# Sigmoid attention and an MLP on one core: blocks of 512 tokens, 64-row scores, float32 products with v, and engine queues written out from a list of tasks

## The chip, the core and the metric

The kernel runs on one core of a Trainium2 chip. The core has TensorE (PE in the profile, with its weight loads as PEld), VectorE (DVE), ScalarE (ACT), GpSimd (POOL, unused here) and SyncE (SP), which issues all DMA transfers. Each engine works through its own queue in order, and engines wait for one another by semaphores. The metric is the device time of one execution in microseconds, the median of several runs.

## The reference

```python
batch, n_heads, seq, head_dim = (8, 12, 448, 64)
scores = scale * np.matmul(q, k.transpose(0, 1, 3, 2)) - np.log(S)     # scale = 1 / sqrt(64), S = 448
attn = 1.0 / (1.0 + np.exp(-scores))
attn_out = np.matmul(attn, v)
x = attn_out.transpose(0, 2, 1, 3).reshape(B * S, H * D)               # 3584 tokens x 768
h = x @ w_in                                                           # w_in 768 x 2048, float64
g = h * (1.0 / (1.0 + np.exp(-1.702 * h)))
out = (g @ w_out).astype(np.float32)                                   # w_out 2048 x 768, float64
```

q, k and v are float32. The weights come to the device as 64-bit words and have to be turned into float32 there.

## The kernel before

**Number formats.** TensorE takes float32 data in two ways here: as fp32r, a rounded format in which one pass does the product, or as plain float32, which the profile shows as two records per product. To keep precision in fp32r, a value is split into a rounded high part and a low part (value minus high part), and a product is the sum of three: low times high, high times low, high times high. Rounding is a copy into an fp32r tile (ScalarE or VectorE), the low part a subtraction on VectorE.

**Weights.** The two matrices are cut into 32 pieces of 128 x 768. The words of a piece are decoded once (`decode_steps`: exponent, bounds, mantissa, low, sign, product; lines 118 to 149) and the float32 result is stored in DRAM (`saved`). The decoding steps are dealt out over the attention of the first batch and the first MLP by `emit`. For each of the 8 batches every piece is loaded (`load_w`, line 161) and split again (`split_w`, lines 168 and 169) into a `wsplit` tile.

**Attention.** It goes head by head. For the first 15 pairs of heads (`NATIVE`) the scores of a chunk of 128 keys are two products on all 128 rows: the high and low parts of k are stacked on the two halves of the rows against q. The probabilities stay float32 and `values_whole` (line 333) multiplies them by v in float32, the two heads of a pair on the two column halves of the array. The other 33 pairs have probabilities and v split into high and low parts (line 313), the scores take seven wide products per head (line 289), and so do the products with v (`values`, line 355), with high and low v side by side on the 128 columns.

**MLP.** It goes batch by batch, on 448 tokens: 16 pieces up (`up`, line 429: 6 k-tiles x 3 products each), sigmoid, product with h, split; then 6 output tiles down (`down`, line 454: 16 x 3 products each). One batch is 576 products of 128 x 128 weights with 448 columns.

**Order.** TensorE's queue is written by hand: attention of the first six pairs comes first, then each batch's MLP with the attention of later pairs dealt between its products (`interleave`, `PAIRS`). SP's queue is by hand in the first part. All the other queues are ordered by the framework's scheduler.

Of the kernel before, what the change touches and what calls it, by code (L numbers as in the profile page):

```python
# [35 lines left out]


def interleave(main, side):

    total_m = sum(c for c, _ in main) or 1.0  # L40
    total_s = sum(c for c, _ in side) or 1.0
    done_m = done_s = 0.0
    n = 0
    units = []
    for c, emit in main:
        units.append((c, emit))
        done_m += c
        while n < len(side) and done_s / total_s < done_m / total_m:
            units.append(side[n])
            done_s += side[n][0]  # L50
            n += 1
    return units + side[n:]
# [3 lines left out]
def sigmoid_attention_mlp(ctx: ExitStack, tc: tile.TileContext, qk, v, w, out):  # L56
# [4 lines left out]
    S = out.shape[3]  # L61
# [3 lines left out]
    NF = NW * NK // (NK + NM)  # L65
    NC = 4
    NW_EL = NK * P
    scale = 1.0 / math.sqrt(D)
    neg_log_s = -math.log(S)

# [6 lines left out]

    bias = const.tile([P, 1], F32, name="bias")
# [5 lines left out]
    def line(name):  # L84
        return sb.tile([P, S], F32, tag="line", name=name, bufs=6)

# [3 lines left out]


    saved = [dram.tile([P, NW_EL], F32, name=f"w{i}", tag=f"w{i}") for i in range(NW)]
    raw64, w32, wsplit = {}, {}, {}
    unsaved = []
    expo, signs = {}, {}

    def load64(n):
        t = sb.tile([P, 2 * NW_EL], F32, tag="a_lo", name=f"w64_{n}", bufs=RAW64).bitcast(U64)
        nc.sync.dma_start(out=t, in_=w[n])
        raw64[n] = t  # L100

    def decode_steps(n):
        def words():
            raw = raw64[n]
            pair = raw.bitcast(U32).rearrange("p (n t) -> p n t", t=2)
            top = raw.bitcast(U16).rearrange("p (n t) -> p n t", t=4)[:, :, 3]
            return pair[:, :, 0], pair[:, :, 1], top

        def mantissa():

            if n + RAW64 - 1 < NW:
                load64(n + RAW64 - 1)
            if n < NF:
                t = sb.tile([P, 2 * S], F32, tag="g", name=f"w32_{n}", bufs=NF)[:, :NW_EL]
            else:
                t = sb.tile([P, NW_EL], F32, tag="wraw", name=f"w32_{n}", bufs=WRAW)
            w32[n] = t
            nc.vector.tensor_scalar(  # L118
                t.bitcast(U32), words()[1], 0xFFFFF, 0x100000, op0=ALU.bitwise_and, op1=ALU.bitwise_or
            )  # L120

        def low():
            t = w32[n]
            nc.vector.scalar_tensor_tensor(  # L124
                t, words()[0], 2.0**-32, t.bitcast(I32), op0=ALU.mult, op1=ALU.add
            )

        def exponent():

            e = sb.tile([P, 8 * D], F32, tag="v", name=f"expo{n}", bufs=NV).bitcast(U16)[:, :NW_EL]  # L130
            expo[n] = e
            t = sb.tile([P, 8 * D], F32, tag="v", name=f"sign{n}", bufs=NV).bitcast(BF16)[:, :NW_EL]
            signs[n] = t
            nc.scalar.activation(t, words()[2].bitcast(I16), AF.Sign)  # L134
            nc.vector.tensor_scalar(e, words()[2], 0x7FF0, None, op0=ALU.bitwise_and)

        def bounds():
            e = expo[n]
            nc.vector.tensor_scalar(e, e, 896.0 * 16, 1151.0 * 16, op0=ALU.max, op1=ALU.min)
            nc.scalar.activation(e, e, AF.Copy, scale=8.0, bias=-896.0 * 128)  # L140

        def sign():
            e, t = expo[n], signs.pop(n)
            nc.vector.tensor_tensor(e.bitcast(BF16), e.bitcast(BF16), t, op=ALU.mult)  # L144

        def product():
            t = w32[n]
            raw64.pop(n)
            nc.vector.scalar_tensor_tensor(
                t, t, 2.0**-20, expo.pop(n).bitcast(BF16), op0=ALU.mult, op1=ALU.mult  # L150
            )
            if n < NF:
                unsaved.append((n, t))
            else:
                nc.sync.dma_start(out=saved[n], in_=t)

        return [(0.55, exponent), (0.6, bounds), (0.55, mantissa), (0.9, low), (0.5, sign), (0.9, product)]

    def load_w(n):
        t = sb.tile([P, NW_EL], F32, tag="wraw", name=f"wraw{n}", bufs=WRAW)  # L160
        nc.sync.dma_start(out=t, in_=saved[n % NW])
        w32[n] = t

    def split_w(n):
        decoding.until(n)
        t = w32.pop(n)
        s = sb.tile([P, 2, NW_EL], F32R, tag="wsplit", name=f"wsplit{n}", bufs=WSPLIT)
        nc.scalar.copy(s[:, 0], t)  # L168
        nc.vector.tensor_tensor(s[:, 1], t, s[:, 0].bitcast(F32), op=ALU.subtract)  # L169
        wsplit[n] = s  # L170

    def ahead(n):

        if NW <= n + WRAW - 1 < B * NW:
            load_w(n + WRAW - 1)
        if n + WSPLIT - 1 < B * NW:
            split_w(n + WSPLIT - 1)

    class Decoding:
        def __init__(self):  # L180
            self.steps = [(c, i, f) for i in range(NW) for c, f in decode_steps(i)]
            self.total = sum(c for c, _, _ in self.steps)
            self.n = 0
            self.done = 0.0

        def step(self):
            c, i, f = self.steps[self.n]
            f()
            self.n += 1
            self.done += c  # L190

        def upto(self, share):
            while self.n < len(self.steps) and self.done < self.total * share:
                self.step()

        def until(self, piece):
            while self.n < len(self.steps) and self.steps[self.n][1] <= piece:
                self.step()

    decoding = Decoding()  # L200


    raw, vraw, parts, vparts, attn, xs, x32s = {}, {}, {}, {}, {}, {}, {}
    heads = [(b, h) for b in range(B) for h in range(H)]

    def native(b, h):
        return (b * H + h) // 2 < NATIVE

    def load_head(b, h):

        mine = qk[b, h * D : (h + 1) * D]
        if native(b, h) or h % 2 == 0:
            t = sb.tile([P, S2], F32, tag="qkraw", name=f"qkraw{b}_{h}", bufs=NQ)
            if native(b, h):
                for j in range(2):
                    nc.sync.dma_start(out=t[j * D : (j + 1) * D], in_=mine)  # L216
            else:
                nc.sync.dma_start(out=t, in_=qk[b, h * D : (h + 2) * D])
                raw[b, h + 1] = t
            raw[b, h] = t  # L220
        if h % 2 == 0:
            t = sb.tile([P, 2, NC, D], F32, tag="vraw", name=f"vraw{b}_{h}", bufs=NVR)
            nc.sync.dma_start(out=t, in_=v[b, :, h : h + 2])
            vraw[b, h // 2] = t

    def split_head(b, h):

        t = raw.pop((b, h))
        s = sb.tile([P, S2 + D + S], F32R, tag="qk", name=f"qk{b}_{h}", bufs=NQK)
        every = slice(0, P)  # L230
        up, dn = slice(0, D), slice(D, P)
        q, k = slice(0, S), slice(S, S2)

        def low(rows, cols, into, src, hi):
            nc.vector.tensor_tensor(s[rows, into], t[src, cols], s[src, hi].bitcast(F32), op=ALU.subtract)  # L235

        if native(b, h):

            if b * H + h < QK_DVE:
                nc.vector.tensor_copy(s[:, :S2], t)  # L240
            else:
                nc.scalar.copy(s[:, :S2], t)  # L242
            low(every, q, slice(S2, S2 + S), every, q)
            low(dn, k, k, dn, k)
        else:


            own, other = (up, dn) if h % 2 == 0 else (dn, up)
            q2 = slice(S2 + D, S2 + D + S)
            full, last = slice(S, S + 3 * P), slice(S + 3 * P, S2)  # L250
            nc.scalar.copy(s[own, :S2], t[own])  # L251
            nc.scalar.copy(s[other, q2], t[own, q])
            low(own, last, slice(S2, S2 + D), own, last)
            low(other, q, q, own, q)
            low(other, full, full, own, full)
            low(own, q, q2, own, q)
            both = slice(S + 3 * P, S2 + D)
            nc.vector.tensor_copy(s[other, both], s[own, both].bitcast(F32))
        parts[b, h] = s
        if not native(b, h):  # L260
            t = vraw[b, h // 2]
            j = h % 2
# [5 lines left out]
    def scores(b, h, half):  # L268
# [23 lines left out]
        if half == 1:  # L292
            parts.pop((b, h))
# [249 lines left out]
```

## Time and profile before

| | |
|---|---|
| median of 3 runs | 1275.14 us (1273.19 to 1276.57) |
| profiled execution, own time | 1273.37 us |
| its span, first to last instruction | 1271.6 us |
| mean granted TensorE clock | 0.998 |
| wide up products, L429 | 2304 records, mean 366 ns |
| wide down products, L454 | 2304 records, mean 366 ns |
| VectorE busy | 967.8 us |
| ScalarE busy | 941.2 us |
| DMA | 179.44 MB, 141 GB/s in the mean, 277 GB/s in the first 60 us |

A row of the windows gives, for a stretch of the span, its length, the busy time of each engine with the number of its records, then the granted clock, the busy share of the DMA engines and what they moved in GB/s. A row of the groups gives line, engine, operation, tiles and shapes, the number of records, then busy time and mean duration, then the engine's idle time before them and what ended it. A row of the chain or of the timeline begins with the start and the duration in us; x counts the records merged into it. A matmul record is longer than the distance to the next one, since they overlap in the array.

### The profile page before, as it was taken

How to read it: one execution, taken by the hardware profiler on the slowest of the kernel's cores; microseconds unless marked ns; L12 is line 12 of the kernel's file. 1: busy time of each engine (PE TensorE's matmuls, PEld its weight loads, DVE VectorE, ACT ScalarE, POOL GpSimd, SP SyncE). 2: the span in 40 equal slices, each digit the busy share in tenths (PEclk: the TensorE clock that was granted, in tenths of full speed). 3: DMA queues.
4: the chain of work that ended last, by engine and by line, in shares of the span. 5: the costliest groups of instructions: out<-in, count | busy, mean ns of one | idle time of the engine just before them, and what ended most of it. 6: DMA issues, size and time to landing. Idle time of an engine off the chain costs nothing.

```text
span 1271.6 us, 17018 instructions
## 1 busy us (share of the span) xinstructions
PE 1241.8 (98%) x6012; PEld 1095.7 (86%) x6012; DVE 967.8 (76%) x1613; ACT 941.2 (74%) x1416; POOL 0.2 (0%) x4
## 2 busy tenths in 40 slices
PE   6899998999999999999999999999999999999998
PEld 3378776789999999999989999999999999999998
DVE  7899988668777897778877888788987778645531
ACT  6878776667778888788878888788888877664531
POOL 0000000000000000000000000000000000000000
PEclk9999999999999999999999999999999999999999
DMA  9976788533434334334334434443334432333342
GB/s 277 282 249 212 217 264 260 180 115 99 128 119 133 111 110 137 123 113 123 113 113 137 131 99 123 128 127 117 110 125 125 127 104 82 110 109 107 112 127 67
DMA packets 64933, 179.44 MB, mean 141 GB/s; under 512 B 7632, under 2 KB 13776, under 8 KB 64848
## 3 DMA queue, kind: packets, MB, share of 16 engines
q1 hardware_dynamic: 64848, 178.35, 45.4%
q8 instruction: 48, 0.79, 0.3%
q14 instruction: 37, 0.30, 0.1%
HBM read 154.73 MB, written 23.59 MB: 140 GB/s over the span
## 4 chain that ended last, share of the span: by engine, by line
PE 90%; DMA 4%; DVE 3%; ACT 1%; issue 1%; SPq 0%; DVEq 0%; ACTq 0%
PE h L429 37%; PE o L454 34%; PE sc L289 9%; PE av L355 7%; DMA w<-w 3%; PE av L333 2%; DMA qkraw<-qk 1%; DVE qk L235 1%; DVE w L124 0%; DVE alo L313 0%; ACT a L296 0%; ACT qk L242 0%; DVE expo L144 0%; DVE w L118 0%; SPq L216 0%
## 5 line engine op out<-in xcount | busy, mean ns | idle before, releaser
L454 PE MATMUL o<-gs,wsplit 128*128 128x448 f32 x2304 | 495.6, 366 | 2.0 <-DVE wsplit L169 1.4
L429 PE MATMUL h<-x,wsplit 128*128 128x448 f32 x2304 | 488.5, 366 | 0.0
L454 PEld LDWEIGHTS o<-gs,wsplit 128*128 128x128 f32 x2304 | 431.8, 188 | 45.8 <-issue 6.3
L429 PEld LDWEIGHTS h<-x,wsplit 128*128 128x128 f32 x2304 | 432.0, 188 | 42.6 <-issue 4.2
L169 DVE TENSOR_TENSOR wsplit<-wraw,wsplit 128x768 fp32r<-128x768 f32 x224 | 213.5, 953 | 76.6 <-ACT wsplit L168 71.6
L168 ACT CAST wsplit<-wraw 128x768 fp32r<-128x768 f32 x224 | 186.2, 831 | 59.9 <-PE o L454 38.7
L313 DVE TENSOR_TENSOR alo<-a,ahi 128x448 fp32r<-128x448 f32 (+1 forms) x132 | 113.1, 856 | 114.7 <-ACT a L296 114.4
L289 PE MATMUL sc<-qk 128*128 128x448 f32 x702 | 177.7, 373 | 19.9 <-ACT a L296 10.8
L296 ACT ACTIVATE a<-sc,bias 128x448 f32<-128x448 f32 (+1 forms) x192 | 166.7, 872 | 20.1 <-PE sc L289 20.1
L235 DVE TENSOR_TENSOR qk<-qkraw,qk 64x64 fp32r<-64x64 f32 (+2 forms) x324 | 164.5, 523 | 16.2 <-ACT qk L251 7.9
L289 PEld LDWEIGHTS sc<-qk 128*128 128x128 f32 x702 | 131.9, 190 | 41.8 <-ACT a L296 20.8
L296 ACT ACTIVATE ahi<-sc,bias 128x448 fp32r<-128x448 f32 (+1 forms) x132 | 108.5, 822 | 66.2 <-DVE rest L302 35.0
L437 ACT ACTIVATE g<-h 128x448 f32<-128x448 f32 x128 | 69.4, 542 | 71.7 <-PE h L429 66.4
L438 DVE TENSOR_TENSOR g<-h,g 128x448 f32<-128x448 f32 x128 | 79.3, 619 | 37.4 <-ACT g L437 35.9
L440 DVE TENSOR_TENSOR gs<-g,gs 128x448 fp32r<-128x448 f32 x128 | 79.0, 618 | 9.7 <-ACT gs L439 8.8
L439 ACT CAST gs<-g 128x448 fp32r<-128x448 f32 x128 | 72.5, 566 | 14.7 <-DVE g L438 13.7
L355 PE MATMUL av<-ahi,v 128*128 128x448 f32 x264 | 64.5, 366 | 0.0
L251 ACT CAST qk<-qkraw 64x896 fp32r<-64x896 f32 x66 | 61.8, 937 | 0.8
L333 PE MATMUL av<-a,vraw 128*64 128x448 f32 (+1 forms) x240 | 55.4, 563 | 2.0 <-DVE x L344 1.0
L355 PE MATMUL av<-alo,v 128*128 128x448 f32 x198 | 52.4, 369 | 2.4 <-DVE alo L313 2.4
L355 PEld LDWEIGHTS av<-ahi,v 128*128 128x128 f32 x264 | 49.6, 188 | 4.2
L134 ACT ACTIVATE sign<-w 128x768 bf16<-128x768 int16 x32 | 29.3, 915 | 26.0 <-DMA w<-w 23.8
(36 smaller groups left out, 746.3 us busy)
## 6 DMA issues: line engine op xcount, KB each, us to landing
wraw<-w SPq DMA_DIRECT2D x224, 384.0 KB, 3.1
w<-w SPq DMA_DIRECT2D x32, 768.0 KB, 6.5
qkraw<-qk SPq DMA_DIRECT2D x33, 448.0 KB, 3.4
qkraw<-qk SPq DMA_DIRECT2D x60, 224.0 KB, 5.4
vraw<-v SPq DMA_DIRECT2D x48, 256.0 KB, 3.2
w<-w SPq DMA_DIRECT2D x32, 384.0 KB, 5.0
out<-osb SPq DMA_DIRECT2D x48, 224.0 KB, 2.0
```

The lines of the kernel that those rows point to most:

```text
L168: nc.scalar.copy(s[:, 0], t)
L169: nc.vector.tensor_tensor(s[:, 1], t, s[:, 0].bitcast(F32), op=ALU.subtract)
L235: nc.vector.tensor_tensor(s[rows, into], t[src, cols], s[src, hi].bitcast(F32), op=ALU.subtract)
L289: nc.tensor.matmul(ps[:, j, :S], lhsT=kk, rhs=s[:, r : r + S], start=n == 0, stop=n == len(terms) - 1)
L296: nc.scalar.activation(out, x, AF.Sigmoid, bias=bias[:rows], scale=scale)
L313: nc.vector.tensor_tensor(out, x, y.bitcast(F32), op=ALU.subtract)
L333: nc.tensor.matmul(ps[j * D : (j + 1) * D, :S], lhsT=vraw[b, p][rows, j, c], rhs=attn[b, 2 * p + j][0][rows, c], start=c == 0, stop=c == N ...
L355: nc.tensor.matmul(ps[:, :S], lhsT=vs[:, c].rearrange("p a d -> p (a d)"), rhs=m, start=n == 0, stop=n == len(todo) - 1,)
L429: nc.tensor.matmul(ps[:, :S], lhsT=ws[a], rhs=x[:, c], start=k == 0 and i == 0, stop=k == NK - 1 and i == 2,)
L438: nc.vector.tensor_tensor(g, ps[:, :S], g, op=ALU.mult)
L440: nc.vector.tensor_tensor(gs[f][:, 1], g, gs[f][:, 0].bitcast(F32), op=ALU.subtract)
L454: nc.tensor.matmul(ps[:, :S], lhsT=ws[a], rhs=gs[f][:, c], start=f == 0 and i == 0, stop=f == NF - 1 and i == 2,)
```

## The change

- **Blocks.** The MLP works on 7 blocks of 512 tokens in place of 8 batches of 448. Attention still goes by batch, and its result is copied into float32 tiles of 512 columns (`to_x`), of which the rounded and low parts are taken.
- **Scores.** They are computed for a pair of heads. Head 0 lies on rows 0 to 63, head 1 on rows 64 to 127; keys go in 4 chunks of 112. A chunk has three terms, and each term is two products on 64 rows, one after the other in the queue, on different row halves of the array and into different banks of the accumulator.
- **Products with v.** All 48 pairs use float32 probabilities and float32 v, as the first 15 did.
- **Weights.** Decoding writes float32 pieces to DRAM. In the second block each piece is read, split, and the split pair is stored (768 KB); from the third block on, the split pair is loaded and nothing is split again.
- **Order.** Every operation becomes a task with a duration, the tasks it needs and the buffers it uses. `Plan.run` plays them through on a clock of its own and emits each at the time it begins, and so writes the queues of TensorE, VectorE, ScalarE and SP. Rounding copies go to ScalarE or VectorE, as the plan finds one free. Attention of the first two batches (12 pairs) precedes the first wide product but for a remainder; then six pairs go with each of the first six blocks, each as one run of scores, four products with v of the pair before, and scores.
- **Removed:** the splitting of probabilities and of v, the stacked k, and the numbers that dealt out the work before.

```diff
-NATIVE = 15
-PAIRS = (9, 5, 6, 6, 6, 6, 4, 0)
-SHARE = 0.7
-EARLY, SPREAD = 7, 0.85
-QK_DVE = 8
-RAW64, WRAW, WSPLIT, NV, NX, NA, NQ, NQK, NVR = 2, 3, 3, 4, 11, 3, 3, 3, 3
+T = 512
+SHARE, LEAD = 0.8, 0.93
+AHEAD = 6
+BUFS = dict(
+    qkraw=2, qk=2, vraw=3, a=4, x32=8, x=6, g=16, line=2, wsplit=3, raw64=2, w32=3, e=3,
+    sc=2, av=1, m=3,
+)
+SIGNAL, LANDING, PER_KB = 0.12, 2.5, 0.0033
...
+    def run(self, streams):
+        for tag, ring in self.rings.items():
+            for n in range(BUFS[tag], len(ring)):
+                ring[n].users[0].deps += ring[n - BUFS[tag]].users
...
+        def pe():
+            if current:
+                return max(free["PE"], current[0].ready), None
+            best = None
+            heads = []
+            if at[1] < len(side):
+                heads.append((1, side[at[1]][1], side[at[1]][0] <= at[0]))
+            if at[0] < len(main):
+                heads.append((0, main[at[0]], True))
+            for s, unit, due in heads:
+                first = [t for t in unit if t.alone]
+                if any(t.left for t in first):
+                    continue
+                when, before = free["PE"], 0.0
+                for t in first:
+                    when = max(when, t.ready - before)
+                    before += t.costs["PE"]
+                if best is None or when < best[0] - 1e-9 or (not best[2] and when <= best[0] + 1e-9):
+                    best = (when, s, due)
+            return (best[0], best[1]) if best else (None, None)
...
+            when, _, e = min(options)
+            if e == "PE":
+                if s is not None:
+                    current += main[at[0]] if s == 0 else side[at[1]][1]
+                    at[s] += 1
+                t = current.pop(0)
+            else:
+                now = [t for t in pools[e] if t.ready <= when]
+                own = [t for t in now if len(t.costs) == 1 or free["ACT"] > when + 1.5]
+                t = min(own if e == "DVE" and own else now, key=lambda t: t.key)
+            t.begun = True
+            count += 1
+            cost = t.costs[e]
+            if e == "SP":
+                free["SP"] = when + 0.08
+                free["DMA"] = max(free["DMA"], when) + cost * PER_KB
+                end = free["DMA"] + LANDING
+            else:
+                end = free[e] = when + cost
+            t.emits[e]()
+            for c in t.then:
+                c.left -= 1
+                c.ready = max(c.ready, end + (0.0 if list(c.costs) == [e] else SIGNAL))
+                if not c.left:
+                    offer(c)
+        return max(free.values())
...
     ps_m = ctx.enter_context(tc.tile_pool(name="ps_m", bufs=3, space=bass.MemoryType.PSUM))
+    ctx.enter_context(tc.manual_schedule(engines={
+        mybir.EngineType.PE, mybir.EngineType.Activation, mybir.EngineType.DVE, mybir.EngineType.SP,
+    }))
...
+    def round_and_rest(costs, b, src, deps, uses, hi, lo, first=lambda: None):
+        c = on_either(
+            (costs[0], lambda: nc.scalar.copy(hi(), src())),
+            (costs[1], lambda: nc.vector.tensor_copy(hi(), src())),
+            deps, [b, *uses], first,
+        )
+        return task(
+            "DVE", costs[2],
+            lambda: nc.vector.tensor_tensor(lo(), src(), hi().bitcast(F32), op=ALU.subtract),
+            [c], [b, *uses],
+        )
...
+        t_e = task("DVE", 0.56, exponent, [load], [e, raw])
+        t_s = task("ACT", 0.92, sign, [load], [sg, raw])
...
+        )
+        t_g = task("DVE", 0.56, lambda: nc.vector.tensor_tensor(
+            e.tile.bitcast(BF16), e.tile.bitcast(BF16), sg.tile, op=ALU.mult), [t_x, t_s], [e, sg])
...
+        t_p = task("DVE", 0.96, lambda: nc.vector.scalar_tensor_tensor(
+            f32(), f32(), 2.0**-20, e.tile.bitcast(BF16), op0=ALU.mult, op1=ALU.mult), [t_l, t_g], [f, e])
+        decoded[n] = (t_p, f, f32)
+        stored[n] = dma(lambda: whole[n], f32, KB, [t_p], [f])
...
+        i = n % NW
+        if n >= 2 * NW:
+            t = dma(lambda: b.tile.bitcast(F32), lambda: halves[i], 2 * KB, [saved[i]], [b], take)
+            return t, b
...
+            f = buffer("w32")
...
+            t = dma(f32, lambda: whole[i], KB, [stored[i]], [f],
+                    lambda: make(f, "w32", [P, NW_EL], F32, f"wraw{n}"))
+            if n < NW and n + AHEAD < NW:
+                decode(n + AHEAD)
...
+        t = round_and_rest((0.83, 0.56, 0.96), b, f32, [t], [f], part(0), part(1), take)
+        if n >= NW:
+            saved[i] = dma(lambda: halves[i], lambda: b.tile.bitcast(F32), 2 * KB, [t], [b])
+        return t, b
...
+    def scores(b, p, c, t_s, s, a):
+        ps = buffer("sc")
+        terms = ((0, 1), (1, 0), (0, 0))
+        def emit():
+            make(ps, "sc", [P, 2, 512], F32, f"sc{b}_{p}_{c}")
+            for n, (kk, qq) in enumerate(terms):
+                for j, rows in enumerate(halves_of_rows):
+                    nc.tensor.matmul(
+                        ps.tile[:C, j, :S],
+                        lhsT=s.tile[rows, kk, S + c * C : S + (c + 1) * C], rhs=s.tile[rows, qq, :S],
+                        start=n == 0, stop=n == len(terms) - 1,
+                    )
+        t = task("PE", 0.65, emit, [t_s], [ps, s])
...
+            nc.scalar.activation(
+                a.tile[:C, c % 2], ps.tile[:C, :, :S], AF.Sigmoid, bias=bias[:C], scale=scale
+            )
...
+    def values(b, p, c, t_a, a, t_v, vr, ps):
+        def emit():
+            if c == 0:
+                make(ps, "m" if b < 2 else "av", [P, 512], F32, f"av{b}_{p}")
+            for j, cols in enumerate(halves_of_rows):
+                nc.tensor.matmul(
+                    ps.tile[cols, :S], lhsT=vr.tile[:C, j, c], rhs=a.tile[:C, c % 2, j],
+                    start=c == 0, stop=c == NC - 1,
+                )
+        return task("PE", 0.8, emit, [t_a, t_v], [ps, a, vr])
...
+    def to_x(b, p, t, ps):
+        for block, into, cols in places(b):
...
+        if b:
+            block = b - 1
+            xb, x = x32[block, p], buffer("x")
+            t = round_and_rest(
+                (0.62, 0.42, 0.69), x, lambda: xb.tile, wrote[block, p], [xb],
+                lambda: x.tile[:, 0], lambda: x.tile[:, 1],
+                lambda: make(x, "x", [P, 2, T], F32R, f"x{block}_{p}"),
+            )
+            xs[block, p] = (t, x)
...
+            if n < 2 * NP:
+                units += [got + (late[i] if late else []) for i, got in enumerate(scored)]
+            else:
+                for t in scored[1]:
+                    t.alone = False
+                units.append(scored[0] + late[0] + late[1] + scored[1])
...
+        def product(ps, w, k, x, first, last):
+            ws = [w[:, i * NW_EL + k * P : i * NW_EL + (k + 1) * P] for i in range(2)]
+            for i, (a, c) in enumerate(((0, 1), (1, 0), (0, 0))):
+                nc.tensor.matmul(
+                    ps, lhsT=ws[a], rhs=x[:, c], start=first and i == 0, stop=last and i == 2
+                )
...
+                t = task(
+                    "PE", 6 * 0.2267, emit, [t_w] + [xs[b, k][0] for k in ks],
+                    [ps, wb] + [xs[b, k][1] for k in ks],
+                )
...
+    side = attention()
+    for n in range(NF + AHEAD):
+        decode(n)
...
+    side = list(zip(due + [due[-1]] * (len(side) - len(due)), side))
+    plan.run((main, side))
```

On TensorE, in the middle of the kernel, the names are sc (scores), av (products with v), h (up), o (down), with the batch or block numbers dropped. Before:

```order
L289 MATMUL sc_7_0_5529<-qk_7_5360 128x448 x3
L429 MATMUL h_10_5548<-x_1_3407,wsplit_5445 128x448 x3
L429 MATMUL h_10_5548<-x_3_3644,wsplit_5445 128x448 x3
L429 MATMUL h_10_5548<-x_5_3944,wsplit_5445 128x448 x3
L429 MATMUL h_10_5548<-x_7_4238,wsplit_5445 128x448 x3
L355 MATMUL av_6_5561<-alo_6_5372,v_6_5224 128x448 x3
L355 MATMUL av_6_5561<-ahi_6_5371,v_6_5224 128x448 x4
L429 MATMUL h_10_5548<-x_9_4485,wsplit_5445 128x448 x3
```

And now, at about the same depth:

```order
L502 MATMUL o_1_5540<-gs_15_5441,wsplit_5556 128x512 x3
L400 MATMUL sc_5_0_5598<-qk_5_5292 112x448 x6
L400 MATMUL sc_5_1_5607<-qk_5_5292 112x448 x6
L423 MATMUL av_4_5617<-a_4_0_5458,vraw_4_5068 64x448 x4
L423 MATMUL av_4_5617<-a_4_2_5497,vraw_4_5068 64x448 x4
L400 MATMUL sc_5_2_5627<-qk_5_5292 112x448 x6
L400 MATMUL sc_5_3_5639<-qk_5_5292 112x448 x6
L502 MATMUL o_2_5648<-gs_0_4921,wsplit_5556 128x512 x3
```

Attention stood in single groups of wide products between wide products; it now stands in one run of half-array products, with four changes of the array's shape around and within it.

On VectorE, early in the first MLP, w and expo are a weight piece in decoding (the number behind w is the piece), wsplit its low part, g and gs the up products' results. Before:

```order
L124 SCALAR_TENSOR_TENSOR w_10_794<-w_10_733,w_10_794 128x768
L135 TENSOR_SCALAR expo_824<-w_11_792 128x768
L438 TENSOR_TENSOR g_4_818<-h_4_785,g_4_818 128x448
L169 TENSOR_TENSOR wsplit_830<-w_7_586,wsplit_830 128x768
L149 SCALAR_TENSOR_TENSOR w_10_794<-w_10_794,expo_769 128x768
L139 TENSOR_SCALAR expo_824<-expo_824 128x768
L118 TENSOR_SCALAR w_11_843<-w_11_792 128x768
L440 TENSOR_TENSOR gs_4_819<-g_4_818,gs_4_819 128x448
```

Now:

```order
L312 TENSOR_TENSOR expo_1015<-expo_1015,sign_1064 128x768
L333 SCALAR_TENSOR_TENSOR w_9_1009<-w_9_1009,expo_1015 128x768
L265 TENSOR_TENSOR gs_0_1091<-g_0_1080,gs_0_1091 128x512
L326 TENSOR_SCALAR w_10_1111<-w_10_1021 128x768
L296 TENSOR_SCALAR expo_1115<-w_10_1021 128x768
L533 TENSOR_TENSOR g_1_1113<-h_1_1069,g_1_1113 128x512
L331 SCALAR_TENSOR_TENSOR w_10_1111<-w_10_1021,w_10_1111 128x768
L265 TENSOR_TENSOR wsplit_1123<-w_4_506,wsplit_1123 128x768
L265 TENSOR_TENSOR gs_1_1127<-g_1_1113,gs_1_1127 128x512
```

Piece 10 was finished after the fifth up product's result (g_4); now piece 9 is finished at the first, g_0, so ten pieces are decoded when the MLP begins.

On SP, w before is a stored piece and wraw its load; now f is a stored float32 piece, w a stored split pair. Before, as the second batch goes on:

```order
L161 DMA wraw_2288<-w_80 128x768
L463 DMA out<-osb_5_2193 128x448
L161 DMA wraw_2318<-w_81 128x768
L161 DMA wraw_2357<-w_82 128x768
L161 DMA wraw_2394<-w_83 128x768
```

Now, at the end of the second block and the start of the third:

```order
L240 DMA wraw_3512<-f_140 128x768
L240 DMA vraw_2_3550<-v 112x512
L240 DMA qkraw_4_3582<-qk 128x896
L240 DMA w_106<-wsplit_3580 128x1536
L240 DMA wraw_3592<-f_141 128x768
L240 DMA out<-osb_3_3601 128x512
L240 DMA w_107<-wsplit_3610 128x1536
L240 DMA w_108<-wsplit_3632 128x1536
L240 DMA w_109<-wsplit_3654 128x1536
L240 DMA out<-osb_4_3664 128x512
L240 DMA wsplit_3680<-w_78 128x1536
L240 DMA wsplit_3700<-w_79 128x1536
```

Single pieces of 384 KB were loaded throughout. In the second block each load now stands in one queue with a store of twice its size, and then split pairs of 768 KB are loaded into the tiles that TensorE reads.

More of the change, by code (lines that the diff above doesn't have):

```diff
@@ L82, in sigmoid_attention_mlp @@
     nc.scalar.activation(warm, bias, AF.Sigmoid)
[L84 to L102, printed above, removed]
+    plan = Plan()
@@ L128, in exponent @@
[L128 to L140, printed above, removed]
@@ L157, in decode_steps @@
[L157 to L170, printed above, removed]
@@ L172, in ahead @@
[L172 to L198, printed above, removed]
```

575 lines of the change are left out of this document (266 added, 309 removed).

## The prediction

> **What bounds the kernel now.** I read the page first, then the windows, the chain of waits in order of time, the waits of TensorE, and the timeline of TensorE around the narrow float32 products.
>
> ```profile
> span 1271.6 us, 17018 instructions
> PE 1241.8 (98%) x6012; PEld 1095.7 (86%) x6012; DVE 967.8 (76%) x1613; ACT 941.2 (74%) x1416; POOL 0.2 (0%) x4
> ...
> 0.00:60.00 60.00, 44.08 (x177) 23.07 (x178) 47.26 (x80) 41.33 (x50) 0.20 (x4) 0.97 0.95 277
> 60.00:272.00 212.00, 204.08 (x965) 158.28 (x963) 181.22 (x303) 154.31 (x212) 0.00 (x0) 1.00 0.69 221
> 272.00:1150.00 878.00, 875.65 (x4294) 805.25 (x4291) 691.89 (x1170) 701.52 (x1086) 0.00 (x0) 1.00 0.38 118
> 1150.00:1272.00 122.00, 118.04 (x583) 109.08 (x581) 47.38 (x63) 44.08 (x69) 0.00 (x0) 0.99 0.34 104
> ```
>
> TensorE is busy 98%, but a busy record overlaps the next, so I count from start to start. The end of the chain is two runs of 288 wide products without a hole:
>
> ```profile
> 1151.31 58.37 PE h L429 x288
> 1209.68 58.38 PE o L454 x288
> 1268.06 0.02 issue
> 1268.08 0.53 ACT osb L462
> ```
>
> 58.37 / 288 = 202.7 ns from one 448-column product to the next. The float32 products with v are cheaper per column than that, and lie in pairs (two column halves of the array, x8 records are four pairs):
>
> ```profile
> 22.56 1.08 PE L289 MATMUL sc<-qk 128*128 128x448 f32 x4 [0.34 <-ACT a L296]
> 23.57 1.72 PE L333 MATMUL av<-a,vraw 128*64 128x448 f32 x8
> 25.22 1.07 PE L289 MATMUL sc<-qk 128*128 128x448 f32 x4
> 26.22 1.87 PE L333 MATMUL av<-a,vraw 128*64 128x448 f32 x8
> ...
> 24.00 0.14 PEld L333 LDWEIGHTS av<-a,vraw 128*64 128x64 f32 x2 [0.23 <-issue]
> 24.37 0.14 PEld L333 LDWEIGHTS av<-a,vraw 128*64 128x64 f32 x2 [0.23 <-issue]
> ...
> L289 PE MATMUL sc<-qk 128*128 128x448 f32 x702 | 177.7, 373 | 19.9 <-ACT a L296 10.8 <-DVE qk L235 9.0
> L333 PE MATMUL av<-a,vraw 128*64 128x448 f32 x180 | 41.9, 564 | 2.0 <-DVE x L344 1.0 <-ACT a L296 0.9
> L333 PE MATMUL av<-a,vraw 64*64 64x448 f32 x60 | 14.5, 562 | 0.0
> ```
>
> A pair passes in 24.37 − 24.00 = 0.37 us (0.375 below: between the rounded ends). Four passes take 1.50 of the 1.65 us from 23.57 to 25.22, and the four wide ones after them 0.81 of the 1.00 us to 26.22. So two changes of the array's shape cost 0.15 + 0.19 = 0.34 us, 0.17 each.
>
> With these prices the span divides. To 272 us there are 1142 records: 240 narrow ones (120 passes, 45.0 us, 60 changes of shape, 10.2 us) and 902 wide ones (182.8 us), 238 in all. The first product starts at 7.3 us (below), so 26.7 us are waits. From 272 to 1150 us 4294 × 0.2027 = 870.4 of 878 us: 7.6 us lost in 878. Then 118.2 of 121.6 us; 3.4 us are the last eviction and store. After 272 us nothing but TensorE's own rate matters, and no relief of VectorE or ScalarE there can be worth more than 7.6 us.
>
> **The change, part by part.**
>
> *Blocks of 512.* 4608 wide products of 448 columns become 7 × 576 = 4032 of 512, the same number of columns. What a 512-column one costs no row shows. The lower end is the float32 pass: 896 columns in 0.375 us is 0.4185 ns a column, 214.3 ns for 512, if what holds the wide product at 202.7 ns is its weight load (188 ns in the row below) and the longer stream covers it. The upper end is proportion, 231.7 ns. The same extra of 15 ns beside the stream gives 229.5. I take 226.5, nearest to the last, because only the 202.7 ns row has these operands; both ends stay. 4032 × 0.2265 = 913.2 us (864 to 934), against 4608 × 0.2027 = 934.0 before.
>
> ```profile
> L454 PEld LDWEIGHTS o<-gs,wsplit 128*128 128x128 f32 x2304 | 431.8, 188 | 45.8 <-issue 6.3
> L355 PE MATMUL av<-ahi,v 128*128 128x448 f32 x264 | 64.5, 366 | 0.0
> L355 PE MATMUL av<-alo,v 128*128 128x448 f32 x198 | 52.4, 369 | 2.4 <-DVE alo L313 2.4
> ```
>
> The Trainium skill ("TensorE: Matmul & The Clock Gate", section "Back-to-back issue gap") gives N/2.4 + 2.5 ns for an isolated gap: 189.2 ns at 448 and 215.8 at 512. This trace has 202.7 at 448, so it disagrees for the wide product; with 215.8 this term would be 870 us.
>
> *Scores on 64 rows.* 702 wide products (142.3 us) become 48 pairs of heads × 4 chunks × 3 terms = 576 couples on the two row halves. If a couple runs side by side as the column halves do, it costs one stream and a few ns: 0.2095 us, 120.7 us in all. No row shows row halves; one after the other, at the wide price, it is 1152 × 0.2027 = 233.5.
>
> *Products with v in float32.* 462 split products (93.6 us, the two L355 rows) and 120 passes (45.0) become 48 × 8 = 384 passes × 0.375 = 144.0 us.
>
> *Changes of shape.* Each pair of heads now has four (wide to row halves, to column halves, back, and out): 192 × 0.17 = 32.6 us, against 10.2. A change between two halved shapes may cost less; with half of them free it is 16.
>
> Sum of TensorE's work: 913.2 + 120.7 + 144.0 + 32.6 = 1210.5 us. Before, by the same prices: 934.0 + 142.3 + 93.6 + 45.0 + 10.2 = 1225.1. The gain by work is only 14.6 us: the blocks give 21, the scores 22, and the products with v and the shapes take 28 back.
>
> *Start and end.* Before:
>
> ```profile
> 5.30 0.63 DVE L240 CAST qk<-qkraw 128x896 fp32r<-128x896 f32 x1 [4.44 <-DMA qkraw<-qk]
> 5.96 1.26 DVE L235 TENSOR_TENSOR qk<-qkraw,qk 128x448 fp32r<-128x448 f32 x2
> 7.28 1.99 PEld L289 LDWEIGHTS sc<-qk 128*128 128x128 f32 x6 [7.28 <-DVE qk L235]
> ...
> L242 ACT CAST qk<-qkraw 128x896 fp32r<-128x896 f32 x22 | 20.7, 939 | 1.2 <-DMA qkraw<-qk 1.2
> L313 DVE TENSOR_TENSOR alo<-a,ahi 128x896 fp32r<-128x896 f32 x66 | 72.1, 1092 | 86.4 <-ACT a L296 86.4
> ```
>
> The new split is one 896-column rounding on ScalarE (0.94) and one 896-column subtraction (1.09), so the first score comes at about 5.3 + 0.94 + 1.09 + signals = 7.6 us. The end stays 3.6.
>
> *Waits to the end of the first block's products.* 26.7 us before. ScalarE and VectorE keep the 32 decodes, the roundings and 72 sigmoids of 896 columns there; what is planned is their order. I take 22 us, bounds 10 and 60 (the second end is the rival below). The later loss stays 8.
>
> *Weights copied as split pairs.* From the third block on, 160 loads of 768 KB replace as many roundings and subtractions (160 × 953 ns = 152 us of VectorE, row L169): nothing on the path, since no wait was left there. But the loads double.
>
> ```profile
> L169 DVE TENSOR_TENSOR wsplit<-wraw,wsplit 128x768 fp32r<-128x768 f32 x224 | 213.5, 953 | 76.6 <-ACT wsplit L168 71.6
> ...
> wraw<-w SPq DMA_DIRECT2D x224, 384.0 KB, 3.1
> w<-w SPq DMA_DIRECT2D x32, 768.0 KB, 6.5
> ```
>
> A 768 KB load lands in 6.5 us in the crowded first stage; with three buffers it has two pieces, 2 × 18 × 0.2265 = 8.2 us. The cover is 1.7 us, and 786 KB per 4.1 us is 193 GB/s of the 277 seen at a share of 0.95. In the second block each piece is read (384 KB) and its split stored (768 KB): with pairs and results about 260 GB/s. I count nothing for both; they are the thinnest covers, and SP's queue stands in line behind any late store.
>
> Sum: 1210.5 + 7.6 + 3.6 + 22 + 8 = 1251.7 us of span. The profiled execution took 1273.37 us for its 1271.6, and the median 1275.14 is 1.8 above it: 1251.7 + 1.8 + 1.8 = 1255 us.
>
> **The rivals.**
>
> *The weight load was the limit.* Then 512 columns cost 214.3 ns and the sum is 1251.7 − 49 = 1202.5, 1206 as a median. For it: the float32 pass, whose two loads are over in 0.14 us, streams without the 15 ns. Against: that pass is another mode of the array. The rule of the Trainium skill named above, in the same section, would give 1209 of span by its 215.8 ns.
>
> *Nothing left.* 229.5 ns and waits as before, 26.7 us: +12 + 5 = 1269 of span, 1272: no change.
>
> *The order of queues turns into waits* (the slower side). By the order, ten of the 32 weight pieces are decoded before the first wide product; the other 22 must come within the first block, 576 × 0.2265 plus six pairs of heads at 12 × 0.2095 + 8 × 0.375 + 4 × 0.17 = 6.2 us, together 168 us, the last one by about 160: 7.3 us a piece.
>
> ```profile
> L99 SPq DMA_DIRECT2D w<-w x32: 328/333/577, 5.7 to 215.6; - x32
> L134 ACT ACTIVATE sign<-w x32: 891/916/947, 13.0 to 221.9; 128x768 bf16<-128x768 int16 x32
> ```
>
> Before, the 32 loads came over 210 us, 6.6 each. A decode needs the sign from ScalarE before VectorE's product, and now takes two of only three such buffers; ScalarE's and VectorE's queues are fixed, so one late sign holds every subtraction behind it. At 9 us a piece the wide products wait 22 × 9 − 160 = 38 us: 1290 of span, 1293. The change is slower than before from 8.2 us a piece.
>
> *The couples of scores do not run side by side.* +113 us: 1365, 1368. The change would then not do what it says. Against it are the narrow products: eight records of 564 ns pass in 1.72 us. The Trainium skill ("TensorEngine Tiling (Array Packing)", section "Key Properties") states that different tiles can load weights and multiply in parallel; for row halves no run here shows it yet.
>
> **How the numbers follow.** Forecast (1235 to 1268) 0.42; weight load the limit 0.20; nothing left 0.08; order of queues 0.20; couples in turn 0.10. About 0.3% is what a measurement of this kernel can tell from no change (1271 to 1279). So faster 0.62, same 0.08, slower 0.30. The range goes from the second case's 1206, less 4, to the order rival at 10 us a piece (22 × 10 − 160 = 60 us, 1315); it leaves out the couples in turn and some 0.06 at the ends.
>
> **What would show it.** Start to start of the wide products, 226.5 ns (214 or 230 decides two rivals); 576 couples at 0.21 us; the first score near 7.6 us; waits of TensorE under 30 us, all before 265 us; none on a weight load after that. I am wrong if TensorE waits for split weights in the first two blocks by more than 40 us, or if the couples take 0.4 us.

## The result, and the profile after

The changed kernel takes 1238.7 us, the median of four runs (1238.39 to 1240.17); the kernel before took 1275.9 beside it. The ratio is 0.9713, with a 95% interval of 0.9693 to 0.9732. The forecast was 1255 us: a gain of 20 us, where 37 came.

From the page, the span and the busy time; from the chain of waits in order of time, its end:

```profile
span 1236.2 us, 14546 instructions
PE 1216.6 (98%) x5952; PEld 900.8 (73%) x5952; DVE 454.3 (37%) x675; ACT 471.1 (38%) x658; POOL 0.2 (0%) x4
```

```profile
1102.02 65.28 PE h L502 x288
1167.30 65.29 PE o L502 x288
1232.60 0.03 ACTq L568
1232.62 0.04 issue
1232.66 0.59 ACT osb L568
```

VectorE's and ScalarE's work has halved, yet TensorE is busy 98% as before: the time is still TensorE's queue. 65.28 / 288 = 226.7 ns is the price of a 512-column product.

The timeline of TensorE in the middle of the kernel shows one run of attention between wide products:

```profile
601.17 1.52 PE L502 MATMUL h<-x,wsplit 128*128 128x512 f32 x6
602.62 1.48 PE L400 MATMUL sc<-qk 64*112 64x448 f32 x12
604.03 3.23 PE L423 MATMUL av<-a,vraw 112*64 112x448 f32 x16
607.19 1.49 PE L400 MATMUL sc<-qk 64*112 64x448 f32 x12
608.61 3.70 PE L502 MATMUL h<-x,wsplit 128*128 128x512 f32 x15
```

Read by the starts: 12 score records, six couples, pass in 1.41 us, and 16 records with v, eight passes, in 3.16. A couple costs 0.2025 us and a pass 0.375 (single records, start to start); the rest, 0.16 to 0.20 us, is the change of shape.

The waits of TensorE are these, all of them:

```profile
PE sc L400 <- DVE qk L265: 6.3, 1, 6.3
PE o L502 <- ACT wsplit L259: 6.1, 1, 6.1
PE av L423 <- ACT x L452: 2.2, 1, 2.2
PE o L502 <- DVE wsplit L265: 1.0, 1, 1.0
PE sc L400 <- ACT a L411: 0.2, 1, 0.2
```

The first is the start (the first score at 6.27 us) and the last lies at 11 us. The other 9.3 us lie between 174 and 194 us: 7.1 us at the first weight piece that is read back from DRAM in the first block, and 2.2 us at a copy of an attention result, which stands behind steps of decoding in ScalarE's queue. Before, some 27 us were lost in that stage.

The waits cost more than their length. The timeline behind them, and the window from 179 to 188 us, with the granted clock third from the end of the row:

```profile
181.40 0.79 PE L502 MATMUL o<-gs,wsplit 128*128 128x512 f32 x1 [6.15 <-ACT wsplit L259]
183.22 6.50 PE L502 MATMUL o<-gs,wsplit 128*128 128x512 f32 x17 [1.02 <-DVE wsplit L265]
189.66 1.48 PE L400 MATMUL sc<-qk 64*112 64x448 f32 x12
```

```profile
179.00:188.00 9.00, 5.57 (x12) 4.10 (x13) 8.62 (x15) 5.59 (x8) 0.00 (x0) 0.50 0.76 244
```

Seventeen products take 6.44 us from start to start, in place of 3.85. At a granted clock of 0.50 single ones start 427 ns apart. The same pace, 0.37 us for a couple of scores, is seen at the very start, until 10.8 us; the windows print a clock of 1.00 there, but the trace has no record of the clock before that time.

```profile
6.27 4.92 PE L400 MATMUL sc<-qk 64*112 64x448 f32 x24 [6.27 <-DVE qk L265]
11.40 1.76 PE L400 MATMUL sc<-qk 64*112 64x448 f32 x12 [0.22 <-ACT a L411]
13.10 1.72 PE L423 MATMUL av<-a,vraw 112*64 112x448 f32 x8
```

These 36 score records take 6.83 us; at the price of the later ones, with one change of shape, it would be some 3.8.

### The profile page after: what moved, and what is told of

It reads as the page before. It is cut to its first block, busy times and chain, and to the rows that moved or that the text cites. A ratio compares the mean times of both kernels' runs of the same rounds, so it can differ in the third digit from the quotient of the medians.

```text
span 1236.2 us, 14546 instructions
## 1 busy us (share of the span) xinstructions
PE 1216.6 (98%) x5952; PEld 900.8 (73%) x5952; DVE 454.3 (37%) x675; ACT 471.1 (38%) x658; POOL 0.2 (0%) x4
## 4 chain that ended last, share of the span: by engine, by line
PE 97%; DVE 1%; ACT 1%; DMA 1%; issue 0%; ACTq 0%
PE h L502 37%; PE o L502 37%; PE av L423 12%; PE sc L400 11%; DMA qkraw<-qk 0%; ACT expo L307 0%; DMA f<-w 0%; DVE w L333 0%; ACT a L411 0%; DVE qk L265 0%; DVE expo L312 0%; ACT qk L259 0%; DVE w L331 0%; ACT sign L300 0%; ACT gs L259 0%
## 5 line engine op out<-in xcount | busy, mean ns | idle before, releaser
L502 PE MATMUL o<-gs,wsplit 128*128 128x512 f32 x2016 | 466.8, 392 | 7.2 <-ACT wsplit L259 6.1
L502 PE MATMUL h<-x,wsplit 128*128 128x512 f32 x2016 | 463.1, 390 | 0.0
L411 ACT ACTIVATE a<-sc,bias 112x896 f32<-112x896 f32 x192 | 183.2, 1005 | 65.0 <-PE sc L400 64.3
L423 PE MATMUL av<-a,vraw 112*64 112x448 f32 x768 | 157.3, 547 | 2.2 <-ACT x L452 2.2
L400 PE MATMUL sc<-qk 64*112 64x448 f32 x1152 | 144.4, 383 | 6.5 <-DVE qk L265 6.3
L400 PEld LDWEIGHTS sc<-qk 64*112 64x112 f32 x1152 | 95.0, 174 | 72.3 <-issue 35.2
L533 DVE TENSOR_TENSOR g<-h,g 128x512 f32<-128x512 f32 x112 | 77.3, 691 | 177.9 <-ACT g L528 177.6
L265 DVE TENSOR_TENSOR gs<-g,gs 128x512 fp32r<-128x512 f32 x112 | 77.4, 691 | 61.8 <-ACT gs L259 61.8
L265 DVE TENSOR_TENSOR wsplit<-wraw,wsplit 128x768 fp32r<-128x768 f32 x48 | 46.0, 958 | 53.3 <-ACT wsplit L259 52.6
L259 ACT CAST wsplit<-wraw 128x768 fp32r<-128x768 f32 x31 | 25.9, 837 | 50.3 <-PE o L502 45.1
```

The lines of the kernel that those rows point to most:

```text
L259: (costs[0], lambda: nc.scalar.copy(hi(), src())),
L265: lambda: nc.vector.tensor_tensor(lo(), src(), hi().bitcast(F32), op=ALU.subtract),
L400: nc.tensor.matmul(ps.tile[:C, j, :S], lhsT=s.tile[rows, kk, S + c * C : S + (c + 1) * C], rhs=s.tile[rows, qq, :S], start=n == 0, stop=n ...
L411: nc.scalar.activation(a.tile[:C, c % 2], ps.tile[:C, :, :S], AF.Sigmoid, bias=bias[:C], scale=scale)
L423: nc.tensor.matmul(ps.tile[cols, :S], lhsT=vr.tile[:C, j, c], rhs=a.tile[:C, c % 2, j], start=c == 0, stop=c == NC - 1,)
L502: nc.tensor.matmul(ps, lhsT=ws[a], rhs=x[:, c], start=first and i == 0, stop=last and i == 2)
```

## The experiments

**Do the 64-row products run side by side, and why?** First the order of the six products of a chunk was changed:

```diff
-            for n, (kk, qq) in enumerate(terms):
-                for j, rows in enumerate(halves_of_rows):
+            for j, rows in enumerate(halves_of_rows):
+                for n, (kk, qq) in enumerate(terms):
```

> The three terms of head 0 come before the three of head 1, so that neighbours in the queue lie on the same row half. If the couples gain by running side by side because neighbours lie on different halves, a chunk takes 5 or 6 streams of 0.2025 us in place of 3: 192 chunks x 0.40 to 0.61 us = 78 to 117 us more, 1317 to 1356 us, and TensorE's score records start about 200 ns apart. If row halves overlap whatever the order in the queue, nothing changes: 1239 us.

1240.8 us (two runs), the same. The timeline of TensorE in this kernel:

```profile
603.43 1.49 PE L400 MATMUL sc<-qk 64*112 64x448 f32 x12
604.84 3.23 PE L423 MATMUL av<-a,vraw 112*64 112x448 f32 x16
```

Twelve records again pass in 1.41 us, and single records still start in twos, 10 ns apart, though the kernel now writes three products of one head ahead of the three of the other. My expectation that neighbours in the kernel's order must alternate was wrong. The records don't name the row half, so whether TensorE starts them out of that order, or they reach it in another, is not shown. Next the row half itself was taken away:

```diff
-                        lhsT=s.tile[rows, kk, S + c * C : S + (c + 1) * C], rhs=s.tile[rows, qq, :S],
+                        lhsT=s.tile[halves_of_rows[0], kk, S + c * C : S + (c + 1) * C], rhs=s.tile[halves_of_rows[0], qq, :S],
```

> Both products of a couple read rows 0 to 63 (head 1's scores are left out, head 0's are computed twice), so that no two neighbours lie on different row halves; number, size and order of the instructions stay. If the couples run side by side because of the two row halves, 576 streams of 0.2025 us are added: 117 us, 1350 to 1360 us, and the score records start about 200 ns apart. If 64-row products are short for another reason, 1239 us.

1362 us (two runs, ratio to the kernel before 1.065, interval 1.060 to 1.070). The same place in its timeline:

```profile
619.81 2.69 PE L400 MATMUL sc<-qk 64*112 64x448 f32 x12
622.43 3.23 PE L423 MATMUL av<-a,vraw 112*64 112x448 f32 x16
```

The 12 records take 2.62 us in place of 1.41: 96 such runs are 116 us, and the spans differ by 1356.2 − 1236.2 = 120. The two row halves, and nothing else about 64-row products, are worth this; in this run the records start one by one, about 200 ns apart.

**What is a 512-column block worth?** Blocks of 448 tokens in the changed kernel (`T = 448`; each block then takes its own batch's attention, and the products read 448 columns of their accumulators):

> Blocks of 448 tokens, all else as in the changed kernel: 4608 wide products in place of 4032. Theory of the sum: 4608 x 0.2027 = 934 us against 4032 x 0.2267 = 914, so 20 us more, 1255 to 1262 us. Rival (the width matters little, the gain came from the attention and the order): within 5 us of 1239.

1272.0 us (ten runs; ratio to the kernel before 0.9974, interval 0.9952 to 0.9995): 33 us more than with 512, 13 beyond the sum. Two pieces of its chain:

```profile
1012.25 23.30 PE o L502 x114
1035.55 58.37 PE h L502 x288
```

The second is 202.7 ns a product; the first, with 0.2 us for the changes of shape at its ends, 202.6. But from about 145 to 1010 us most single steps are 206.7 ns: about 949 us from wide product to wide product in all, where 4608 × 0.2027 is 934. The 448-column product has two prices. The kernel before has them too; two runs of 30 products, both from its chain:

```profile
302.41 6.20 PE h L429 x30
...
407.05 6.08 PE h L429 x30
```

6.20 / 30 = 206.7, 6.08 / 30 = 202.7. To see whether these stretches belong to a place in the program, the kernel before was run again as it is.

> The kernel before, unchanged, for a second profile. Its wide products ran at 206.7 ns in some stretches and 202.7 in others, 8 us in all, which the forecast carried over as a loss of the chip. If the stretches belong to the 448-column product in this program, they come back at the same places of the span (about 280 to 360 and 540 to 660 us). If they belong to that one execution, they lie elsewhere or are gone.

1273.4 us, and its chain has, at the place that ran at 202.7 in the first profile:

```profile
408.01 6.20 PE h L429 x30
```

The slower stretch now goes from 280 to about 510 us, and the one from 510 to 660 us is gone. So between about 355 and 660 us the price differs between two executions of the same program, and elsewhere it does not. It is not the granted clock, which reads 1.00 in stretches of either price; what sets it stays open. With 512 columns the runs of wide products in the chain had 226.7 ns wherever the granted clock was 1.00.

A much narrower product tells a constant from a floor. `W = 256`, and the products and what follows use `[:, :W]`:

> The wide products and what follows them use only the first 256 of a block's 512 columns (the other half of the MLP is left out). Read from start to start within a piece. If a product costs its stream and a constant 13 to 16 ns (226.7 at 512, 202.7 at 448), 256 columns take 120 to 123 ns. If the weight load of 188 ns sets a floor, they take 190 to 205 ns. If a load only holds its way in for 107 ns (first load to the second one in a group), the floor is under the stream, again 120.

From its timeline, within a piece whose weights are there:

```profile
701.42 2.68 PE L503 MATMUL o<-gs,wsplit 128*128 128x256 f32 x21
```

Less the last record's own 0.28 us, 20 steps take 2.40 us: 120.0 ns. 256 columns at 120.0 and 512 at 226.7 are 0.4167 ns a column and 13.3 ns beside; 448 would then be 200.0 and measures 202.7 or 206.7. The weight load, a record of 188 ns at 512 columns and 197 ns in the mean here, does not set a floor: it is longer than this step. Where the granted clock was 0.50, single steps are 213.5 ns at 256 columns, 373.5 at 448 and 427 at 512: 0.833 ns a column, and nothing beside. So what stands beside the columns at the full clock is not a fixed cost of each product; what it is stays open. This kernel's whole time, 941.8 us in one run, is no result, since loads of weights then set the pace.

**Is relieving VectorE and ScalarE worth time?** The stored split pairs were taken out, so that each of seven blocks reads float32 pieces and splits them:

```diff
-        if n >= 2 * NW:
+        if n >= NB * NW:
...
-        if n >= NW:
+        if n >= NB * NW:
             saved[i] = dma(lambda: halves[i], lambda: b.tile.bitcast(F32), 2 * KB, [t], [b])
```

> Every block reads the float32 piece and splits it again; the stored split pairs are gone. Theory of the sum (TensorE's queue is the time): VectorE gets 160 x 0.958 us and ScalarE about as much again, but none of it is waited for after the first block: 1239 us, within 4. Rival (the gain came from relieving VectorE and ScalarE): at least 10 us come back, 1249 or more, as waits of the wide products for split weights.

1238.3 us (four runs, 1237.7 to 1238.8), no difference. The window from 430 to 1100 us, first of this kernel, then of the changed one:

```profile
430.00:1100.00 670.00, 670.00 (x3248) 502.04 (x3247) 299.82 (x409) 253.58 (x353) 0.00 (x0) 1.00 0.35 105
```

```profile
430.00:1100.00 670.00, 670.00 (x3248) 502.41 (x3247) 146.16 (x215) 201.52 (x289) 0.00 (x0) 1.00 0.55 181
```

VectorE has 154 us more to do in the same 670 us, and DMA moves 105 GB/s in place of 181; TensorE's column is the same to the record. The converse, in the kernel before (`NATIVE = 48`):

> The kernel before with all 48 pairs of heads in float32 products with v and scores on 128 rows: that part of the change without the row halves, the blocks and the plan. Theory of the sum: 33 pairs go from 28 x 0.2027 = 5.68 us to 16 x 0.2027 + 8 x 0.375 + 2 x 0.34 = 6.92 us, so 41 us more: 1308 to 1325 us, although VectorE and ScalarE lose the splitting of probabilities. Rival (relief of VectorE and ScalarE is worth time): 1275 us or less.

1321.4 us (two runs; ratio 1.033, interval 1.029 to 1.038): 43 to 46 us more than the kernel before, where the sum had 41, although VectorE's work falls from 968 to 654 us. Float32 products with v cost time by themselves; the row halves pay for them.

**What is the written order worth?** The framework was left to order VectorE, ScalarE and SP, then only the first two, then only SP:

```diff
-        mybir.EngineType.PE, mybir.EngineType.Activation, mybir.EngineType.DVE, mybir.EngineType.SP,
+        mybir.EngineType.PE,
```

> Only TensorE's queue stays as the plan wrote it; the framework's scheduler orders VectorE, ScalarE and SP, as before the change. If the planned order of those three queues is what took some 17 us of waits out of the first stage, these come back: 1250 to 1260 us, with the waits before 265 us of the span. If the plan of TensorE's queue alone does it, 1239 us, within 4.

> TensorE and SP as planned, VectorE and ScalarE ordered by the framework. With all three free 38 us were added, 27 of them as scores waiting for ScalarE's sigmoids. If the order on VectorE and ScalarE is the cause, most of it stays: 1265 to 1278 us. If SP's order was, this comes to 1239 to 1245 us.

> TensorE, VectorE and ScalarE as planned, SP ordered by the framework. If the order on VectorE and ScalarE carries the gain, 1237 to 1245 us. If SP's order is the cause (a load of weights ahead of a load of q and k or of a reload), 1260 to 1278 us.

1277.2 us with all three free (ratio 1.002, interval 1.000 to 1.003), 1291.3 with the two (1.012, 1.008 to 1.015), 1246.9 with SP alone (0.978, 0.975 to 0.981). So the order on VectorE and ScalarE carries it, by more than I had expected, and SP's carries 8 us. The two don't add up: with SP free as well the time is 14 us less than with SP as planned. With TensorE's queue as planned, the change without the written order of the two engines gains nothing; whether another queue of TensorE would suit the framework's order was not tried. The first stage of the second kernel, on ScalarE and on TensorE:

```profile
16.32 0.83 ACT L259 CAST wsplit<-w 128x768 fp32r<-128x768 f32 x1 [3.18 <-DVE w L333]
17.06 1.00 ACT L411 ACTIVATE a<-sc,bias 112x896 f32<-112x896 f32 x1
```

```profile
12.30 2.58 PE L400 MATMUL sc<-qk 64*112 64x448 f32 x12 [1.86 <-ACT a L411]
18.12 1.46 PE L400 MATMUL sc<-qk 64*112 64x448 f32 x6 [3.23 <-ACT a L411]
```

The rounding of a weight piece, which nobody needs yet, stands ahead of a sigmoid on ScalarE and waits 3.18 us for that piece to be decoded; the next scores have no accumulator until the sigmoid is done, and TensorE waits 3.23 us. Over this kernel TensorE's waits for sigmoids add up to 33.1 us:

```profile
PE sc L400 <- ACT a L411: 33.1, 14, 8.2
```

The longest, 8.2 us, has the same cause: ahead of a sigmoid, the sign of a weight piece waits 9.36 us for VectorE. In the changed kernel the same stretch of ScalarE is sigmoids with one other step between them, and TensorE waits 0.2 us. All waits of TensorE, the start aside, are 44.3 us against 9.5; the spans differ by 54. Much of the rest goes with the clock:

```profile
60.00:265.00 205.00, 174.75 (x864) 110.59 (x865) 146.06 (x234) 127.49 (x177) 0.00 (x0) 0.92 0.57 193
```

It is 0.92 in the mean from 60 to 265 us, against 0.98 in the changed kernel, and the slow pace of the start lasts until 22 us in place of 10.8.

**The waits that are left.** The reload of piece 16 shares three float32 buffers with the decoding, six pieces ahead.

```diff
-AHEAD = 6
+AHEAD = 3
```

> AHEAD 3 in place of 6. TensorE's last waits (10 us between 174 and 194 us) fall on the first reloaded piece: the three float32 buffers are shared by decoding and reloading, and with AHEAD 6 the reload of piece 16 takes the buffer of piece 19, so that it starts after 19 is decoded and stored (171.05 + 3.04, reload at 175.37). With 3 it waits for piece 16 alone. If that ring is the cause, 4 to 9 us go: 1230 to 1235 us. If VectorE's and ScalarE's pace of decoding is the cause, the waits move to later pieces: 1237 to 1241 us.

1232.7 us (six runs; ratio to the kernel before 0.9646, interval 0.9617 to 0.9675): 6 us less, as the ring theory had it, though 4.6 us of waits are left on later pieces. Then a fourth buffer:

```diff
-    qkraw=2, qk=2, vraw=3, a=4, x32=8, x=6, g=16, line=2, wsplit=3, raw64=2, w32=3, e=3,
+    qkraw=2, qk=2, vraw=2, a=4, x32=8, x=6, g=16, line=2, wsplit=3, raw64=2, w32=4, e=3,
```

> AHEAD 3 and four float32 buffers in place of three (v loads give up one of three). Some 5 us of waits are left with AHEAD 3, between 179 and 242 us, on reloaded pieces that chain store, reload and split. A fourth buffer lets the reload run one piece earlier: 1228 to 1232 us. If VectorE's pace is what holds them, 1231 to 1234 us, no change against AHEAD 3.

1225.8 us (five runs, 1225.5 to 1225.9; ratio 0.9611, interval 0.9584 to 0.9638), 13 us under the changed kernel and 7 under the one with three buffers, more than expected: not only the 4.6 us of waits are gone but the slower clock with them (0.83 from 220 to 230 us there, 1.00 here). Its page, its waits of TensorE and the place where the wait was:

```profile
span 1224.0 us, 14542 instructions
```

```profile
PE sc L400 <- DVE qk L265: 6.2, 1, 6.2
```

```profile
167.75 1.75 PE L502 MATMUL h<-x,wsplit 128*128 128x512 f32 x7
169.33 2.88 PE L502 MATMUL o<-gs,wsplit 128*128 128x512 f32 x12
172.15 1.48 PE L400 MATMUL sc<-qk 64*112 64x448 f32 x12
```

The start is the only wait left, and the first down products follow the up products without a hole. This version beats both kernels; but for the start and the end, what is left of its time is TensorE's own.

## Why the prediction was right, and where its sizes were off

The forecast's case came true: faster, by TensorE's queue, with the wide product at 226.7 ns (forecast 226.5), passes of 0.375 us, and couples side by side. By its own sum, in us of span:

| term | forecast | measured |
|---|---|---|
| 4032 wide products | 913.2 | 914.0 (× 0.2267) |
| 576 couples of scores | 120.7 | 116.6 (× 0.2025) |
| 384 passes with v | 144.0 | 144 (× 0.375) |
| changes of shape | 32.6 | about 36 (190 of 0.19 in the mean) |
| start, end | 7.6, 3.6 | 6.3, 3.6 |
| slow first scores | | 3 (36 records in 6.83) |
| waits in the first stage | 22 | 12 (span against that of the last version, which has none) |
| later loss | 8 | none seen |
| not explained | | 1 |
| span | 1251.7 | 1236.2 |

Three steps were mis-sized, all to the same side, so that the gain is nearly twice the forecast.

- **"The later loss stays 8."** I read those 8 us as a loss of the chip and carried them over. Some 4.5 us of them were the second price of the 448-column product, 206.7 ns over about 240 us, and went with that width. Another 2.4 us stand in the row of L355 in the prediction itself, as waits for the low part of the probabilities (alo, L313), and went with that split; so it was not quite true that nothing but TensorE's rate mattered there. For the first reason "the blocks give 21" was short: with 448 tokens the changed kernel takes 33 us more. The error was to put one row, the clean 202.7 ns at the end, in place of the product's steps all along the span.
- **"I take 22 us"** for the waits of the first stage, a number between bounds with nothing under it. The 26.7 us that it started from were not all waits, as the prediction has it: TensorE's list of waits before has 16.4 us in that stage, the start aside, and part of the rest is slow products, such as the first nine at about 0.37 us. The written order left 12 us, 9.3 of them waits and the rest the low clock behind them. The experiments show that this term was the widest of all: 53 us lie between two orders of VectorE and ScalarE for the same instructions.
- **Couples at 0.2095 us.** The few ns for the second stream, taken over from the column halves, are not there; a couple costs one wide product.

The rivals: "nothing left" fell with 226.7 ns and the shorter waits. "The weight load was the limit" fell twice, by 226.7 ns in the changed kernel and by 120.0 ns at 256 columns. The isolated gap in the Trainium skill ("TensorE: Matmul & The Clock Gate", section "Back-to-back issue gap") has the right slope, N/2.4, but 2.5 ns beside it where these products show 13.3. "The couples do not run side by side" fell, and its price was right: 113 us forecast, 120 (spans) to 123 (medians) measured when they cannot. "The order of queues turns into waits" did not happen, but its mechanism is real: the framework's order on two engines is 1291 us, almost the 1293 that I gave that rival, though by chance: its place was the scores at the start rather than the decoding in the first block. The decoding did hold TensorE, for 12 us with the low clock, by the buffers that I named only as a thin cover elsewhere.

That copying split pairs is worth nothing on the path was right (1238.3 without it). The covers that I called the thinnest held: a 768 KB load of split weights landed in 4.3 us, against 8.2 available.

```profile
wsplit<-w SPq DMA_DIRECT2D x160, 768.0 KB, 4.3
```

## What to carry to other kernels

Where one engine is busy 98%, price its queue instruction by instruction, start to start, and over the whole span: here the gain of the scores and the cost of the products with v, with their changes of shape, nearly cancelled, and a 2% second price of one shape was worth some 5 us. The order of the engines that are half idle still decides: one step that waits, ahead of a sigmoid, stops TensorE two engines away, and TensorE's granted clock was low behind the longer stops. After such a change, ask of every wait that is left which ring of buffers it is; here one more buffer and a smaller lead were worth 13 us.

## What the runs showed of the hardware

- Products on the two row halves overlap: they start in twos, 10 ns apart or less, and 12 take 1.41 us in place of 2.62. They do so even when the kernel writes three of one half ahead of three of the other. The Trainium skill ("TensorE: Matmul & The Clock Gate", Part 3, "The mechanism") states strict order of starts and ends; the records don't name the half, so no run here shows whether that holds.
- A product of 128 × 128 rounded float32 weights costs 0.4167 ns a column and 13.3 ns more at 256 and 512 columns; at 448 it has two prices, 202.7 and 206.7 ns, that change in the course of an execution at a granted clock of 1.00. At 0.50 it costs 0.833 ns a column and nothing more (213.5, 373.5 and 427 ns).
- In a wait of 6.15 us, from 175 to 181 us, the granted clock fell to 0.50 and stayed there until 188 us, and 17 products took 6.44 us in place of 3.85; in the version without waits it stayed at 1.00. How long a wait has to be was not tested.
- A change of the array's shape costs TensorE 0.15 to 0.23 us, the first weight load that nothing covers included.
